# Output products of two gated layers in float16 parts, with divided high weights and low parts kept 1024 times larger

## The chip, the core and the metric

The kernel runs on one core of a Trainium2 chip. It uses five engines with queues of their own: TensorE (PE; a weight load is PEld), VectorE (DVE), ScalarE (ACT), GpSimd (POOL) and SyncE (SP), which issues the transfers here. An engine takes its instructions in the order of the program; a wait for another engine is a semaphore. The metric is the device time of one execution in microseconds.

## What is computed

```python
def _attn_ref(q, k, v, f):               # (4, 8, 576, 64), f: (4, 8, 576)
    scores = 1.0 / np.sqrt(D) * np.matmul(q, k.transpose(0, 1, 3, 2))
    cum = np.cumsum(np.log(np.clip(f, 0.0001, 1.0)), axis=-1)
    scores = np.where(causal, -1000000000.0, scores + cum[:, :, :, None] - cum[:, :, None, :])
    attn = softmax(scores)
    return np.matmul(attn, v)

def _moe_ref(x, w_a, w_b, w_out):        # 2304 tokens, 512 -> 1536 -> 512
    return ((x @ w_a) * (x @ w_b)) @ w_out

def _moe2_ref(x, w_in, w_out):           # 512 -> 2048 -> 512
    h = x @ w_in
    g = np.where(h >= 1, h, np.where(h <= -1, 0.0, (h + 1) ** 2 / 4.0))
    return g @ w_out
```

Attention over 32 heads (the kernel's 4 batches of 8 heads are cut in the reference's order), then the first layer (called the first mixture here), then the second. Inputs are float32 with a wide range of values; the weights come to the chip as pairs of 32-bit words that the kernel decodes to float32.

## The kernel before

**Products in parts.** A matmul of full precision is made of three: high weight by high activation, high weight by low activation, low weight by high activation (`mm3`, lines 590 to 594; in the profile L592, L593 and L594). For the input products (`whi_in`, `wlo_in`, activations `xh` and `xl` in the tile `xhl`) the parts are float16: a weight unit (four blocks of 128 x 128) is scaled by a power of two from its largest magnitude, `sc`, so that it fits; `winv` is the inverse scale. For the output products (`whi_out`, `wlo_out`, activations `ah`, `al`) the parts are float32 with the type fp32r, unscaled.

**Weights.** `weight_stream` decodes units in pairs: a transfer (`wraw`), two passes on ACT, three on DVE and one on POOL (`decode`, L509 to L519). For an input pair, the maximum of each unit (`wmx`, L568) is transposed on PE (L476), reduced on DVE, spread over all partitions by a small matmul on PE (L489), and inverted (`wsc`). `split_unit` then makes the parts: of an input unit ACT makes the high part (L534) and POOL scales (L535) and subtracts (L536); of an output unit POOL copies (L538) and subtracts (L539). The stream is advanced by `w_pump` every second tick of the main loop and whenever a block is asked for that is not there yet; finished units stand in rings, which `w_free` makes free.

**Items.** Tokens are cut into five spans of 460 or 464. An item is one group of hidden features by one span. In the first mixture (`moe1_item`, groups of two features' blocks) the two input products `oa` and `ob` are multiplied: ACT scales `oa` to `asb` (L652), DVE multiplies with `ob` (L653), ACT casts the result to `ah` (L654), POOL subtracts to get `al` (L655). In the second (`moe2_item`, groups of four) DVE clamps (L732), ACT squares (L733), DVE scales and takes the maximum (L734), ACT casts to `ah` (L735), POOL subtracts to `al` (L736); the scales of an item (`ih`, `ihalf`, `htop`, `hlow`) are operations of 4 columns on DVE (L720 to L723). The output products of an item (`out_part`) are issued within the next item: in the first mixture behind that one's first feature, in the second behind its third of four. `accumulate` adds them into `y` (DVE, L691 and L768; a copy on ACT for the first group) or, in the last group, writes the result out (L771).

**Order.** Up to the end of attention all instructions go through `Plan`, which collects them and issues them in an order that a model of the engines makes; where that model has PE idle it puts filler matmuls (`heat`, L1053, on a constant `mask`), and its instructions have the line L304. There one group of the first mixture for each batch, with spans of 288, is threaded between attention rounds. Behind it (`xpose` of the last batch, L1026 to L1037, then the items of all further groups) the tile framework's scheduler sets the order of each engine. Products of an item use six PSUM banks there; one while `Plan` orders.

Of the kernel before, what the change touches and what calls it, by code (L numbers as in the profile page):

```python
# [55 lines left out]
F64_MAX = 122864.0  # L56

# [267 lines left out]
def tile_decay_attention__then__moe__then__moe2(  # L325
# [45 lines left out]
    half = const.tile([P, 1], F32, name="half")  # L371
# [59 lines left out]
    def constants():  # L431
# [18 lines left out]
        nc.gpsimd.memset(half, 0.5)  # L450
# [71 lines left out]
    def split_unit(u, m):  # L522
        k = kind(u)
        while not free[k]:
            yield False
        free[k] -= 1
        p = slot(k)
        dt = F16 if k == "in" else F32R
        hi = p.tile([P, UB, P], dt, name=f"whi_{k}", tag=f"whi_{k}")
        lo = p.tile([P, UB, P], dt, name=f"wlo_{k}", tag=f"wlo_{k}")  # L530
# [12 lines left out]
    def weight_stream():  # L543
# [5 lines left out]
        for u0 in range(0, NU + 2, 2):  # L549
            new = wdec_p.tile([P, 2, UB * P], F32, name="wm", tag="wm") if u0 < NU else None  # L550
            scaled = u0 > 0 and kind(u0 - 2) == "in"
# [14 lines left out]
            if u0 < NU and kind(u0) == "in":  # L566
# [10 lines left out]
    def w_block(i):  # L577
# [3 lines left out]
        hi, lo = ws[u]  # L581
        return hi[:, i % UB, :], lo[:, i % UB, :]
# [22 lines left out]
    def act_pair(nt):  # L605
        return tuple(env["act"].tile([P, env["width"]], F32R, name=n, tag=n)[:, :nt] for n in ("ah", "al"))
# [27 lines left out]
    def scale_of(u, b):  # L634

        if (u, b) not in xw:
            t = xw_p.tile([P, 2], F32, name="xw", tag="xw")
            nc.vector.tensor_scalar(t, winv[:, u:u + 2], xinv[:, b:b + 1], None, ALU.mult)
            xw[u, b] = t
        return xw[u, b]  # L640

    def moe1_item(g, b, c0, nt, last_use):
# [5 lines left out]
        def epilogue(oa, ob, ic):  # L648
# [3 lines left out]
            nc.scalar.activation(asb, oa, AF.Copy, scale=ic[:, 0:1])  # L652
            after(4, lambda: nc.vector.scalar_tensor_tensor(pr, ob, ic[:, 1:2], asb, ALU.mult, ALU.mult))  # L653
            after(5, lambda: nc.scalar.copy(ah, pr))  # L654
# [539 lines left out]
```

## Time and profile before

| | |
|---|---|
| median of 3 runs | 1058.06 us |
| lowest, highest | 1055.68 us, 1067.14 us |
| span of the profiled execution | 1063.1 us |
| PE matmul, busy | 1034.0 us, 97% of the span |
| PE weight load, busy | 736.8 us, 69% |
| DVE, busy | 712.5 us, 67% |
| ACT, busy | 510.9 us, 48% |
| POOL, busy | 543.0 us, 51% |
| granted PE clock, mean | 0.984 of full speed |

The profile is of one execution. For that execution the page gives the span, from its first to its last instruction, and no time of another kind. Busy times count the durations of instructions, and those of successive matmuls overlap; how fast matmuls follow each other is read from their starts. A row of a group gives the busy time of all its instructions and their mean duration, then how long the engine stood idle just before them and what ended that. A row of the timeline gives start, duration, engine, line, operation, what is written and read, and the shape.

### The profile page before, as it was taken

Reading aid. Unit: us, or ns where it says so; the run is one execution under the profiler, and the core shown is the slowest. Engines: PE = TensorE matmul, PEld = TensorE weight load, DVE = VectorE, ACT = ScalarE, POOL = GpSimd, SP = SyncE. Lnnn points to the kernel's source line nnn. Section 1 sums busy time; section 2 is a strip of 40 time slices with the busy share of each in tenths; the row PEclk is TensorE's granted clock in tenths of the full one; section 3 lists DMA queues with packets and bytes.
Section 4 is the critical chain, followed back from the end, with each engine's and each line's share of the span. In section 5 each row is a group of like instructions: output and inputs, shape, how many; then the busy total and the mean of one; then the engine's idle time right before and its main releaser. Section 6 shows DMA issues by size and latency. Waiting matters only on the chain.

```text
span 1063.1 us, 17972 instructions
## 1 busy us (share of the span) xinstructions
PE 1034.0 (97%) x6799; PEld 736.8 (69%) x6799; DVE 712.5 (67%) x1584; ACT 510.9 (48%) x957; POOL 543.0 (51%) x516
## 2 busy tenths in 40 slices
PE   6999999889999999999999999999999999999998
PEld 5788888778765666666666666666766766767766
DVE  7699999977768663562753688964378567654342
ACT  4699888677654341331332444554445335223231
POOL 6388988654368651642723733732366347324121
PEclk8699999989999999999999999999999999999999
DMA  9454555321033220120210211010022011000101
GB/s 246 142 167 133 162 167 155 112 79 39 24 98 86 71 82 1 40 80 1 62 59 8 92 60 40 22 58 1 1 80 80 1 40 40 1 1 11 62 37 71
DMA packets 22054, 72.00 MB, mean 68 GB/s; under 512 B 2776, under 2 KB 5336, under 8 KB 21904
## 3 DMA queue, kind: packets, MB, share of 16 engines
q1 hardware_dynamic: 21968, 70.87, 22.2%
q8 instruction: 53, 0.87, 0.3%
q14 instruction: 33, 0.27, 0.1%
HBM read 60.26 MB, written 5.96 MB: 62 GB/s over the span
## 4 chain that ended last, share of the span: by engine, by line
PE 73%; DVE 15%; ACT 4%; issue 3%; DMA 3%; POOL 2%; SPq 0%; DVEq 0%; ACTq 0%; POOLq 0%
PE mm L592 21%; PE mm L594 20%; PE mm L593 20%; PE s L304 4%; DVE prob L304 3%; PE tp L304 3%; DVE tl L304 3%; PE mm L304 3%; PE o L304 2%; DMA wraw<-in_w_dram 1%; DVE xt L304 1%; DVE wm L516 1%; ACT prob L304 1%; DVE wm L512 1%; DVE wm L514 1%
## 5 line engine op out<-in xcount | busy, mean ns | idle before, releaser
L592 PE MATMUL mm<-xhl,whi_in 128*128 128x460 f16 (+2 forms) x752 | 266.8, 355 | 0.0
L593 PE MATMUL mm<-xhl,whi_in 128*128 128x460 f16 (+2 forms) x752 | 266.5, 355 | 0.0
L594 PE MATMUL mm<-xhl,wlo_in 128*128 128x460 f16 (+2 forms) x752 | 266.5, 355 | 0.0
L592 PE MATMUL mm<-ah,whi_out 128*128 128x460 f32 (+2 forms) x536 | 198.6, 384 | 0.6 <-ACT ah L735 0.6
L736 POOL TENSOR_TENSOR al<-tmp,ah 128x460 fp32r<-128x460 f32 (+1 forms) x80 | 96.2, 1203 | 201.0 <-ACT ah L735 200.9
L593 PE MATMUL mm<-al,whi_out 128*128 128x460 f32 (+2 forms) x536 | 197.8, 370 | 0.8 <-POOL al L736 0.8
L594 PE MATMUL mm<-ah,wlo_out 128*128 128x460 f32 (+2 forms) x536 | 197.6, 370 | 0.0
L655 POOL TENSOR_TENSOR al<-tmp,ah 128x460 fp32r<-128x460 f32 (+2 forms) x54 | 64.9, 1203 | 139.5 <-ACT ah L654 121.0
L592 PEld LDWEIGHTS <-whi_in 128*128 128x128 f16 x752 | 73.4, 98 | 75.1 <-issue 9.4
L594 PEld LDWEIGHTS <-wlo_in 128*128 128x128 f16 x752 | 73.5, 98 | 69.5
L593 PEld LDWEIGHTS <-whi_in 128*128 128x128 f16 x752 | 73.6, 98 | 64.7 <-issue 0.2
L733 ACT ACTIVATE tmp<-tmp,half,ihalf 128x460 f32<-128x460 f32 (+1 forms) x80 | 61.7, 771 | 113.3 <-DVE tmp L732 109.1
L592 PEld LDWEIGHTS mm<-ah,whi_out 128*128 128x128 f32 x536 | 100.4, 188 | 15.7 <-ACT ah L735 1.0
L593 PEld LDWEIGHTS mm<-al,whi_out 128*128 128x128 f32 x536 | 100.7, 188 | 12.3 <-POOL al L736 1.1
L519 POOL TENSOR_TENSOR wm<-wm,wr 128x512 int32<-128x512 int32 x58 | 75.4, 1300 | 64.9 <-DVE wm L516 48.1
L594 PEld LDWEIGHTS mm<-ah,wlo_out 128*128 128x128 f32 x536 | 100.7, 188 | 10.8
L653 DVE SCALAR_TENSOR_TENSOR tmp<-mm,xw,tmp 128x460 f32<-128x460 f32 (+2 forms) x54 | 36.7, 680 | 97.8 <-PE mm L594 96.5
L734 DVE SCALAR_TENSOR_TENSOR tmp<-mm,ih,tmp 128x460 f32<-128x460 f32 (+1 forms) x80 | 55.5, 694 | 51.8 <-ACT tmp L733 49.4
L732 DVE TENSOR_SCALAR tmp<-mm,htop,hlow 128x460 f32<-128x460 f32 (+1 forms) x80 | 59.9, 749 | 43.0 <-PE mm L594 42.7
L304 ACT ACTIVATE prob<-prob,nm 128x512 f32<-128x512 f32 (+4 forms) x144 | 80.4, 586 | 14.2 <-DVE nm L304 13.0
L735 ACT CAST ah<-tmp 128x460 fp32r<-128x460 f32 (+1 forms) x80 | 46.1, 576 | 66.5 <-DVE tmp L734 58.4
L304 PE MATMUL tp<-ident,prob 128*128 128x128 f32 x400 | 74.5, 291 | 2.5 <-ACT prob L304 0.8
(163 smaller groups left out, 2040.6 us busy)
## 6 DMA issues: line engine op xcount, KB each, us to landing
wraw<-in_w_dram SPq DMA_DIRECT2D x68, 512.0 KB
raw<-in_qk_dram SPq DMA_DIRECT2D x26, 608.0 KB
vraw<-in_v_dram SPq DMA_DIRECT2D x16, 320.0 KB
qk<-q SPq DMA_DIRECT2D x28, 160.0 KB
out_dram<-tmp SPq DMA_DIRECT2D x16, 230.0 KB
cum_d<-xhl SPq DMA_DIRECT2D x1, 1216.0 KB
y<-in_qk_dram SPq DMA_DIRECT2D x2, 608.0 KB
out_dram<-tmp SPq DMA_DIRECT2D x4, 232.0 KB
```

The costliest lines, as they stand in the source:

```text
L304: getattr(getattr(self.nc, engine), method)(*a, **kw)
L519: nc.gpsimd.tensor_tensor(t, t, r, ALU.add)
L592: nc.tensor.matmul(o, lhsT=wh, rhs=xh, start=first, stop=False)
L593: nc.tensor.matmul(o, lhsT=wh, rhs=xl, start=False, stop=False)
L594: nc.tensor.matmul(o, lhsT=wl, rhs=xh, start=False, stop=last)
L653: after(4, lambda: nc.vector.scalar_tensor_tensor(pr, ob, ic[:, 1:2], asb, ALU.mult, ALU.mult))
L655: after(6, lambda: nc.gpsimd.tensor_tensor(al, pr, V(ah), ALU.subtract))
L732: nc.vector.tensor_scalar(t, o, top[:, m], low[:, m], ALU.min, ALU.max)
L733: after(1, lambda: nc.scalar.activation(t, t, AF.Square, scale=ihalf[:, m], bias=half))
L734: after(2, lambda: nc.vector.scalar_tensor_tensor(r, o, ih[:, m], t, ALU.mult, ALU.max))
L735: after(3, lambda: nc.scalar.copy(ah, r))
L736: after(4, lambda: nc.gpsimd.tensor_tensor(al, r, V(ah), ALU.subtract))
```

## The change

Weights of the output products are now scaled and split as those of the input products are, both parts in float16. A third tile, `wdown`, is the high part divided by 1024 (`LOW`), made on DVE. `mm3` takes it for the product with the low activation. Activations are scaled by a bound that is known before the product (for the first mixture from the weights' scales, `group1`; for the second from `group2` and the span's scale), `ah` is float16 and holds the activation divided by 1024, `al` is float16 and holds what remains, not divided. `split_act` makes them with two scaled copies on ACT and the subtraction on POOL. `accumulate` multiplies by a scale (`out_scale1`, `osc`). The scales of an item of the second mixture are made by five operations on DVE and six on POOL.

```diff
+LOW = 2.0 ** 10
...
-    half = const.tile([P, 1], F32, name="half")
...
-        dt = F16 if k == "in" else F32R
...
-        if k == "in":
-            sc = wsc[:, u:u + 1]
-            nc.scalar.activation(hi, t, AF.Copy, scale=sc)
-            nc.gpsimd.tensor_scalar(t, t, sc, 0.0, ALU.mult, ALU.add)
-            nc.gpsimd.tensor_tensor(lo, t, hi, ALU.subtract)
-        else:
-            nc.gpsimd.tensor_scalar(hi, t, 1.0, 0.0, ALU.mult, ALU.add)
-            nc.gpsimd.tensor_tensor(lo, t, V(hi), ALU.subtract)
-        ws[u] = (hi, lo)
+        sc = wsc[:, u:u + 1]
+        nc.scalar.activation(hi, t, AF.Copy, scale=sc)
+        nc.gpsimd.tensor_scalar(t, t, sc, 0.0, ALU.mult, ALU.add)
+        nc.gpsimd.tensor_tensor(lo, t, hi, ALU.subtract)
+        down = hi
+        if k == "out":
+            down = p.tile([P, UB, P], F16, name="wdown", tag="wdown")
+            nc.vector.tensor_scalar(down, hi, 1.0 / LOW, None, ALU.mult)
+        ws[u] = (hi, lo, down)
...
-            scaled = u0 > 0 and kind(u0 - 2) == "in"
+            scaled = u0 > 0
...
-            if u0 < NU and kind(u0) == "in":
+            if u0 < NU:
                 mx = const2.tile([P, 2], F32, name="wmx", tag="wmx")
...
-        wh, wl = wb
+        wh, wl, wd = wb
         nc.tensor.matmul(o, lhsT=wh, rhs=xh, start=first, stop=False)
-        nc.tensor.matmul(o, lhsT=wh, rhs=xl, start=False, stop=False)
+        nc.tensor.matmul(o, lhsT=wd, rhs=xl, start=False, stop=False)
         nc.tensor.matmul(o, lhsT=wl, rhs=xh, start=False, stop=last)
...
+    def split_act(ah, al, r, spare, delay):
+        def high():
+            nc.scalar.activation(ah, r, AF.Copy, scale=1.0 / LOW)
+            nc.scalar.activation(spare, ah, AF.Copy, scale=LOW)
+
+        after(delay, high)
+        after(delay + 1, lambda: nc.gpsimd.tensor_tensor(al, r, spare, ALU.subtract))
...
+    def out_scale1(g, b):
+        if ("o", g, b) not in xw:
+            u = base1[g] // UB + 4
+            t, o = small("ot", 2), small("os", 2)
+            nc.vector.tensor_scalar(t, group1(g)[0], xinv[:, b:b + 1], 2.0 ** 31, ALU.mult, ALU.mult)
+            nc.vector.tensor_scalar(t[:, 0:1], t[:, 0:1], t[:, 1:2], 2.0, ALU.mult, ALU.mult)
+            nc.vector.tensor_scalar(o, winv[:, u:u + 2], t[:, 0:1], None, ALU.mult)
+            xw["o", g, b] = o
+        return xw["o", g, b]
...
-            after(5, lambda: nc.scalar.copy(ah, pr))
-            after(6, lambda: nc.gpsimd.tensor_tensor(al, pr, V(ah), ALU.subtract))
+            split_act(ah, al, pr, asb, 5)
...
+            w_block(ob + KC * nf - 1)
+            sc = out_scale1(g, b)
...
-            nc.vector.tensor_tensor(ys, o, ys, ALU.add)
+            nc.vector.scalar_tensor_tensor(ys, o, sc, ys, ALU.mult, ALU.add)
...
-        nc.vector.tensor_scalar(ih, winv[:, u0:u0 + 4], yinv[:, i:i + 1], None, ALU.mult)
...
+        nc.gpsimd.tensor_scalar(ih, winv[:, u0:u0 + 4], yi, 0.0, ALU.mult, ALU.add)
+        nc.vector.tensor_scalar(u, yi, group2(g), 1.0, ALU.mult, ALU.add)
...
         nc.vector.reciprocal(top, ih)
-        nc.vector.tensor_scalar(low, top, -1.0, None, ALU.mult)
-        nc.vector.tensor_scalar(ihalf, ih, 0.5, None, ALU.mult)
+        nc.gpsimd.tensor_scalar(low, top, -1.0, 0.0, ALU.mult, ALU.add)
+        nc.gpsimd.tensor_scalar(mid, rv, 16.0, 0.0, ALU.mult, ALU.add)
+        nc.gpsimd.tensor_scalar(ihalf, ih, rv, 16.0, ALU.mult, ALU.mult)
+        nc.gpsimd.tensor_scalar(full, ihalf, rv, 64.0, ALU.mult, ALU.mult)
...
-            after(3, lambda: nc.scalar.copy(ah, r))
-            after(4, lambda: nc.gpsimd.tensor_tensor(al, r, V(ah), ALU.subtract))
+            split_act(ah, al, r, t, 3)
...
+            nc.gpsimd.tensor_scalar(osc, winv[:, ob // UB:ob // UB + 4], v, v, ALU.mult, ALU.mult)
```

On PE, at the end of an output part in the last group of the second mixture, before (weights, then the input unit of the next products):

```order
L592 MATMUL mm<-ah,whi_out 128x460
L593 MATMUL mm<-al,whi_out 128x460
L594 MATMUL mm<-ah,wlo_out 128x460
L592 LDWEIGHTS whi_in_205
L592 MATMUL mm<-xhl,whi_in_205 128x464
L593 LDWEIGHTS whi_in_205
```

and at the same place now:

```order
L589 LDWEIGHTS whi_out
L589 MATMUL mm<-ah,whi_out 128x460
L590 LDWEIGHTS wdown
L590 MATMUL mm<-al,wdown 128x460
L591 LDWEIGHTS wlo_out
L591 MATMUL mm<-ah,wlo_out 128x460
L589 LDWEIGHTS whi_in_199
```

Each output matmul has a weight load of its own now, as the input matmuls had and have; the order of the three is the same, and the low activation meets `wdown`.

On ACT, within an item of the second mixture in the third of its four groups, where weights are decoded, before (`wm` is the decoded unit, `w` its maximum, `tmp` the clamped and squared activation):

```order
L733 ACTIVATE tmp<-tmp,half,ihalf 128x460
L492 COPY winv<-tp 128x2
L534 ACTIVATE whi_in<-wm_192,wsc 128x512 x2
L735 CAST ah<-tmp 128x460
L733 ACTIVATE tmp<-tmp,half,ihalf 128x460
```

and around an output unit in the same group now:

```order
L775 ACTIVATE tmp<-tmp,hmid,ihalf 128x460
L491 COPY winv<-tp 128x2
L531 ACTIVATE whi_out_215<-wm_186,wsc 128x512
L531 ACTIVATE whi_out_218<-wm_186,wsc 128x512
L636 ACTIVATE ah<-tmp 128x460
L775 ACTIVATE tmp<-tmp,hmid,ihalf 128x460
L637 ACTIVATE tmp<-ah 128x460
L636 ACTIVATE ah<-tmp 128x460
L637 ACTIVATE tmp<-ah 128x460
```

The cast has become two copies (L636 and L637), and between two of them the next item's square can stand; high parts of output units (L531 with `whi_out`) are ACT's now.

On POOL, where items of the third group run and no input unit is left to split, before:

```order
L736 TENSOR_TENSOR al<-tmp,ah 128x460 x6
L736 TENSOR_TENSOR al<-tmp,ah 128x464 x4
L736 TENSOR_TENSOR al<-tmp,ah 128x460 x2
L538 TENSOR_SCALAR whi_out<-wm_192 128x512
L539 TENSOR_TENSOR wlo_out<-wm_192,whi_out 128x512
```

and now:

```order
L640 TENSOR_TENSOR al<-tmp 128x460 x4
L795 TENSOR_SCALAR hos<-winv,hv 128x4 x2
L762 TENSOR_SCALAR hlow<-htop 128x4
L763 TENSOR_SCALAR hmid<-hrv 128x1
L764 TENSOR_SCALAR ihalf<-ih,hrv 128x4
L765 TENSOR_SCALAR hfull<-ihalf,hrv 128x4
L640 TENSOR_TENSOR al<-tmp 128x460
```

Between the four `al` of an item stand operations of 1 or 4 columns now, in the same queue.

## Rows read from the trace of the kernel before

**Rows 1.** The page's first row: span of the profiled execution.
```profile
span 1063.1 us, 17972 instructions
```

**Rows 2.** Stretches: us, then each engine's busy us (instructions), PE clock, DMA share, GB/s.
```profile
0.00:283.00 283.00, 260.40 (x2892) 218.83 (x2893) 247.19 (x795) 212.94 (x445) 187.40 (x200) 0.94 0.45 132
60.00:220.00 160.00, 148.61 (x1809) 126.61 (x1808) 155.36 (x510) 132.78 (x285) 131.68 (x124) 0.99 0.49 148
283.00:655.00 372.00, 371.63 (x1921) 237.22 (x1919) 221.51 (x376) 141.66 (x258) 188.53 (x171) 1.00 0.18 54
655.00:707.00 52.00, 50.46 (x252) 31.68 (x251) 48.89 (x93) 29.67 (x54) 28.70 (x24) 1.00 0.20 61
707.00:1059.00 352.00, 351.54 (x1738) 249.02 (x1738) 194.06 (x321) 126.60 (x202) 138.41 (x123) 1.00 0.09 29
```

**Rows 3.** PE's waits, 275 us to end: what waited, for what, total us, times, longest.
```profile
PE mm L593 <- POOL al L736: 0.8, 1, 0.8
PE mm L592 <- ACT ah L735: 0.6, 1, 0.6
PE tp L489 <- ACT wdg L483: 0.5, 1, 0.5
```

**Rows 4.** Timeline of PE: start us, duration us, line, operation; first and last of three runs.
```profile
1016.97 0.37 PE L593 MATMUL mm<-al,whi_out 128*128 128x460 f32 x1
...
1026.52 0.37 PE L594 MATMUL mm<-ah,wlo_out 128*128 128x460 f32 x1
...
1029.08 0.36 PE L592 MATMUL mm<-xhl,whi_in 128*128 128x464 f16 x1
...
1035.93 0.36 PE L594 MATMUL mm<-xhl,wlo_in 128*128 128x464 f16 x1
...
1036.55 0.37 PE L594 MATMUL mm<-ah,wlo_out 128*128 128x460 f32 x1
...
1045.97 0.37 PE L594 MATMUL mm<-ah,wlo_out 128*128 128x460 f32 x1
```

**Rows 5.** Groups by form: line, tiles, shape, count, busy us, mean ns, idle before.
```profile
L592 PE MATMUL mm<-ah,whi_out 128*128 128x460 f32 x416 | 154.2, 385 | 0.6 <-ACT ah L735 0.6
...
L592 PE MATMUL mm<-ah,whi_out 128*128 128x464 f32 x104 | 40.3, 391 | 0.0
...
L304 PE MATMUL mm<-ah,whi_out 128*128 128x288 f32 x48 | 16.0, 333 | 0.1
```

**Rows 6.** Timeline of PE around one spreading matmul, three rows in succession.
```profile
796.62 0.36 PE L594 MATMUL mm<-xhl,wlo_in 128*128 128x460 f16 x1
796.91 0.17 PE L489 MATMUL tp<-wdg,ones 2*128 2x2 bf16 x1
797.01 0.37 PE L592 MATMUL mm<-xhl,whi_in 128*128 128x460 f16 x1
```

**Rows 7.** Groups by form of the nearest operations; last, one line's min/median/max in ns.
```profile
L735 ACT CAST ah<-tmp 128x460 fp32r<-128x460 f32 x64 | 36.8, 575 | 52.7 <-DVE tmp L734 47.2 <-PE mm L594 4.7 <-DVE w L480 0.8
...
L534 ACT ACTIVATE whi_in<-wm,wsc 128x512 f16<-128x512 f32 x36 | 24.6, 718 | 9.5 <-PE mm L593 9.4
...
L568 DVE TENSOR_REDUCE wmx<-wm 128x2 f32<-128x1024 f32 x17 | 20.7, 1215 | 8.8 <-POOL wm L519 8.8
...
L512 DVE TENSOR_SCALAR wm<-wm 128x512 f32<-128x512 f32 x58 | 40.6, 700 | 17.4 <-ACT wm L509 17.2
...
L720 DVE TENSOR_SCALAR ih<-winv,yinv x20: 208/221/1199, 631.5 to 974.3; 128x4 f32<-128x4 f32 x20
```

**Rows 8.** Timeline: fourth `al` on POOL and its first matmul on PE, two items.
```profile
822.94 1.18 POOL L736 TENSOR_TENSOR al<-tmp,ah 128x460 fp32r<-128x460 f32 x1 [4.20 <-ACT ah L735]
...
824.31 0.37 PE L593 MATMUL mm<-al,whi_out 128*128 128x460 f32 x1
...
1013.13 1.16 POOL L736 TENSOR_TENSOR al<-tmp,ah 128x460 fp32r<-128x460 f32 x1 [11.19 <-ACT ah L735]
...
1018.83 0.37 PE L593 MATMUL mm<-al,whi_out 128*128 128x460 f32 x1
```

More of the change, by code (lines that the diff above doesn't have):

```diff
@@ L580, in w_block @@
             assert w_pump()
-        hi, lo = ws[u]
-        return hi[:, i % UB, :], lo[:, i % UB, :]
+        return tuple(t[:, i % UB, :] for t in ws[u])
     def w_free(u):
@@ L605, in act_pair @@
     def act_pair(nt):
-        return tuple(env["act"].tile([P, env["width"]], F32R, name=n, tag=n)[:, :nt] for n in ("ah", "al"))
+        return tuple(env["act"].tile([P, env["width"]], F16, name=n, tag=n)[:, :nt] for n in ("ah", "al"))
     pending = []
@@ L632, in tile_decay_attention__then__moe__then__moe2, with small, group1, group2 @@
     base2 = [end1 + i * 4 * 2 * KC for i in range(len(G2))]
[L634 to L640, printed above, removed]
+    def small(name, n=1):
+        return xw_p.tile([P, n], F32, name=name, tag=name)
+    def split_act(ah, al, r, spare, delay):
[4 more added lines that the diff above has]
+        after(delay + 1, lambda: nc.gpsimd.tensor_tensor(al, r, spare, ALU.subtract))
+    def group1(g):
+        if ("g", g) not in xw:
+            u = base1[g] // UB
+            top, inv, q, r = small("gtop", 2), small("ginv", 2), small("gq", 4), small("gr", 2)
+            nc.vector.tensor_tensor(top, winv[:, u:u + 2], winv[:, u + 2:u + 4], ALU.max)
+            nc.vector.reciprocal(inv, top)
+            for i in range(2):
+                nc.vector.tensor_tensor(q[:, 2 * i:2 * i + 2], winv[:, u + 2 * i:u + 2 * i + 2], inv, ALU.mult)
+                nc.vector.tensor_scalar(r[:, i:i + 1], q[:, 2 * i:2 * i + 1], q[:, 2 * i + 1:2 * i + 2], 2.0 ** -27,
+                                        ALU.mult, ALU.mult)
+            xw["g", g] = (top, r)
+        return xw["g", g]
+    def out_scale1(g, b):
[7 more added lines that the diff above has]
+        return xw["o", g, b]
+    def group2(g):
+        if ("k", g) not in xw:
+            u = base2[g] // UB
+            k = small("gk")
+            nc.vector.tensor_reduce(k, winv[:, u:u + 4], axis=AX.X, op=ALU.max)
+            nc.vector.tensor_scalar(k, k, 2.0 ** 39, None, ALU.mult)
+            xw["k", g] = k
+        return xw["k", g]
     def moe1_item(g, b, c0, nt, last_use):
@@ L646, in moe1_item, with epilogue @@
         acts = []
-        def epilogue(oa, ob, ic):
+        def epilogue(oa, ob, r):
             asb, pr = tmp(nt), tmp(nt)
@@ L764, in accumulate @@
             ys = y[:, c, cs]
+            sc = osc[:, c:c + 1]
             if g == 0:
-                nc.scalar.copy(ys, o)
+                nc.scalar.activation(ys, o, AF.Copy, scale=sc)
             elif g < len(G2) - 1:
-                nc.vector.tensor_tensor(ys, o, ys, ALU.add)
+                nc.vector.scalar_tensor_tensor(ys, o, sc, ys, ALU.mult, ALU.add)
             else:
                 t = tmp(nt)
-                nc.vector.tensor_tensor(t, o, ys, ALU.add)
+                nc.vector.scalar_tensor_tensor(t, o, sc, ys, ALU.mult, ALU.add)
                 nc.sync.dma_start(out=out[c * P:(c + 1) * P, cs], in_=t)
@@ L1125, in tile_decay_attention__then__moe__then__moe2 @@
     xw_p = pool("xw2", 4)
+    xw.clear()
     env["pt"] = pool("ps_t2", 2, space=bass.MemoryType.PSUM)
```

31 lines of the change are left out of this document (18 added, 13 removed).

## The prediction

> **What bounds the kernel now.** I read the page first, then the busy time by stretches, then what TensorE waits for, then its timeline matmul by matmul. The page gives a span of 1063.1 us [rows 1]. The stretches divide it: up to 283 us (attention, with the first group of the first mixture threaded in) PE has 260.4 of 283 us and DVE 247.2; from 283 us to 1059 us PE has 371.6 of 372, 50.5 of 52 and 351.5 of 352 [rows 2]. After 275 us the waits of PE that the profile can name are of 0.8, 0.6 and 0.5 us, once each [rows 3]. So the last three quarters of the kernel last exactly as long as PE's own stream of matmuls, and a change there is worth what it does to the pace of that stream. Ahead of 283 us the bound is mixed: from 60 us to 220 us DVE is the fullest engine (155.4 of 160 us) [rows 2].
>
> The reader should then see two paces in that stream. In a run of output products with fp32r operands, 47 matmuls of 460 columns start between 1016.97 and 1026.52 us: 46 steps in 9.55 us, 207.6 ns each; in the next run, 1036.55 to 1045.97 us, 45 steps take 209.3 ns each. Input products in float16, 464 columns wide, take 35 steps from 1029.08 to 1035.93 us: 195.7 ns each, which is 194.0 ns for 460 columns [rows 4]. The duration that a group shows for one matmul (385 ns) overlaps its neighbours and is not the pace [rows 5].
>
> **What the change removes.** Every output product becomes a float16 matmul with a weight load of its own, three per block as before. Taking 208.5 ns as the mean of the two fp32r runs, one wide output matmul is shortened by 14.5 ns. There are 416 + 104 of each of three kinds [rows 5], 1560 in all, and the loads do not come out as extra time, because the float16 input products already carry one load per matmul and still run at 194 ns. That is 22.6 us. 64 narrow ones (288 columns) after 283 us at the same saving give 0.9 us. Together −23.5 us, all of it on the engine that sets the end. Of the 48 narrow ones per kind ahead of that [rows 5], the same saving would be 2 us, if PE set the end there.
>
> Here the page "TensorE: Matmul & The Clock Gate" of the Trainium skill, section "Back-to-back issue gap", speaks against the change: warm matmuls follow each other every N/2.4 + 2.5 ns, and no type of operand is in it, so that fp32r and float16 should run alike. For 460 columns that is 194.2 ns, which this trace agrees with for float16, and disagrees with for fp32r; by the page the −23.5 us would be nothing.
>
> **What it adds on TensorE.** Output weights are now scaled as the input weights are, so each pair of output units brings a transpose of its maxima and a small spreading matmul. The order of the two programs holds 30 such pairs of the later kind where it held 17: 13 more. One spreading matmul between input products stretches a step of 0.195 us to 0.39 us (796.62 to 797.01 us) [rows 6], a pause of 0.195 us; I put the transpose between nothing and the same, so a pair costs 0.195 to 0.39 us, and I take 0.3: 13 × 0.3 = +3.9 us (2.5 to 5.1).
>
> **What it adds on the other engines, after 283 us.** For each of 130 activations ScalarE now does two scaled copies where it did one cast of 575 ns [rows 7]: about 75 us more over 776 us, in which ScalarE was busy 298 us [rows 2]; no bound, but a longer chain from the last input product of an item to the low part `al` that the output product needs. An output unit goes from a GpSimd copy to a ScalarE copy (718 ns), and VectorE gets the maximum of each pair (1215 ns) and the divided weight `wdown`; no row has that operation, the nearest is a scaling of as many float32 elements on VectorE, 700 ns on the mean [rows 7]. I keep 0 and 1.4 us (twice that row) as ends, and 0.7 as value. The four small steps of a spread come to 4 × 0.22 = 0.9 us at the median of the small scaling `ih` [rows 7]. For 13 pairs that is 13 × (1.2 + 2 × 0.7 + 0.9) = 13 × 3.5 = 45 us of VectorE beside 776 us, in which it has 464 us [rows 2]. Accumulating with a scale, and the cost of the raised maxima, lie beside PE's matmuls in the same way. If that cover were gone, what waits is PE at the first use of a weight.
>
> What can come out on PE is a wait for `al`. In a quiet item the fourth `al` ends at 1014.29 us and its matmul starts at 1018.83 us, 4.5 us later; while weights are decoded, one ends at 824.12 us for a matmul at 824.31 us, 0.2 us later [rows 8]. The added copy takes about 0.6 us of that. The timeline has 20 items of the second mixture; the last is ordered in another way, and of the other 19 five have less than 3 us to spare. None late is 0; all 20 late by 0.6 us is 12 us. From 655 us to 707 us VectorE is busy 48.9 of 52 us [rows 2]; two pairs of output units passing there add 2 × 3.5 = 7 us, which can be put off to the emptier stretch behind it, or be met by PE. I take 3.5 us for both, close to the end with slack, since 14 of the 19 items have it: +3.5 (−1.9, if the present waits go, to 12).
>
> **Up to 283 us.** VectorE gets one pair of output units (3.5 us) and some 14 more small scalings (0.22 us at the median of `ih`) [rows 7]: 6.6 us, of which a part lies where VectorE is 97% busy. Of the fillers that the program's planner puts where it expects PE idle, the order holds 183 instead of 139, which says that PE's work there moves, not what it costs. ScalarE gets 28 narrow copies. PE may give back 2 us. Between −2 and +7 us I take +2, since the end of this stage, from 220 us on, is PE's again.
>
> **Sum.** −23.5 + 3.9 + 3.5 + 2 = −14.1 us. The profiled span of 1063.1 us becomes 1049.0. That span lies within the runs shown (1055.68 to 1067.14 us), 5.0 us over their median of 1058.06; taken off the median, 1044.0 us.
>
> **Rivals.**
> *All hidden.* No `al` late, the present waits gone, PE's gain kept up to 283 us: −23.5 + 2.5 − 1.9 − 2 = −24.9, or 1033 us. For it: slack of over 4 us in most items. Against: the stretch from 655 us, where VectorE has no room.
> *Given back.* PE's stream is shorter, but its waits take it: −23.5 + 5.1 + 12 + 7 = +0.6, or 1059 us. For it: VectorE at 97% in 60 to 220 us and 94% in 655 to 707 us.
> *Slower: GpSimd's small operations hold up `al`.* Each item of the second mixture now has five operations of 4 columns on GpSimd ahead of its fourth `al`, in one queue. No row has them; the same scaling on VectorE takes 208 to 1199 ns, half of them up to 221 [rows 7]. If each took 1.2 us, 6 us plus 0.6 of copy would exceed the 4.5 us of slack by 2.1 us in each of 20 items: 42 us, and with the rest −14.1 + 42 = +28, 1086 us. It decides from 1.6 us an item, that is from about 1.1 us for one such operation. Against it: GpSimd waits for the cast ahead of the `al` in most items, and the small ones need not wait for it.
> The page "SBUF — State Buffer" of the Trainium skill, section "SBUF: two separate sides", says that VectorE and GpSimd take one shared pair of ports by turns, each for a whole instruction; no row here tells which of two held the other, but the spread of the small scaling would fit it.
> *No gain in pace.* If the pace of the output products did not follow their type, what is added would stay alone: 3.9 + 3.5 + 2 = +9.4, or 1067 us. Against it: the two paces of one trace, 14.5 ns apart, ten microseconds apart. That rival is the rule of the skill's page on TensorE, above.
>
> **How the numbers follow.** The forecast, 1044 us with its own range of 1038 to 1051, gets 0.50; all hidden 0.17; given back 0.20; slower 0.08; no gain in pace 0.05. A change of 1%, 10.6 us, is about what a measurement of this kernel can tell from none: faster means below 1047.5 us, slower above 1068.6 us. Three quarters of the forecast's own chance and all of "all hidden" lie below: 0.375 + 0.17, or 0.55. Slower takes the 0.08 of its rival and a little of the two next to it: 0.10. The rest, 0.35, is within 1%. The range runs from all hidden to given back, 1033 to 1059 us, and leaves out the two last rivals and some of the edges.
>
> **What would show it.** Right: output matmuls of 460 columns that start 194 ns apart; PE without idle time between 283 us and the end but for a few microseconds near the change from the first to the second mixture; last PE instruction some 16 us earlier counted from the first input product behind attention. Wrong: waits of PE for `al` in many items (slower, or given back), waits of PE on the spreading matmuls, a first stage longer than 290 us, or output matmuls still at 208 ns. The forecast would fall with the first stage above all, whose order of instructions is remade as a whole and which no row of before can tell.

## The result, and the profile after

The changed kernel takes 1051.47 us at the median of 18 runs (1038.03 to 1057.21), the kernel before 1058.11 us over 18 runs on the same chip (1055.68 to 1068.0). The ratio is 0.990, 95% interval 0.987 to 0.993. Medians here are over all runs, while a ratio leaves disturbed runs out and is not the quotient of the medians; where the two differ, the text says so.

The time lies inside the range, 7.5 us above the forecast of 1044.0. The profiled run of the changed kernel took 1044.85 us, and that agreement is half chance, as the experiments show. Its page begins with the span (before: [rows 1]) and the busy time of each engine:

```profile
span 1043.1 us, 18612 instructions
PE 1010.7 (97%) x6871; PEld 594.1 (57%) x6871; DVE 736.0 (71%) x1761; ACT 600.4 (58%) x1159; POOL 584.7 (56%) x635
```

The stretches, with the columns of [rows 2] (us, then busy us of PE, PEld, DVE, ACT, POOL with their instructions, PE clock, DMA share, GB/s):

```profile
0.00:281.00 281.00, 257.32 (x2939) 213.21 (x2939) 253.10 (x817) 219.81 (x461) 188.76 (x199) 0.96 0.46 133
60.00:220.00 160.00, 147.05 (x1720) 123.12 (x1719) 152.98 (x492) 132.53 (x283) 121.51 (x115) 0.97 0.46 137
281.00:655.00 374.00, 373.40 (x1984) 191.40 (x1982) 243.71 (x479) 175.73 (x341) 192.81 (x182) 1.00 0.18 54
655.00:700.00 45.00, 41.77 (x214) 20.39 (x213) 39.90 (x96) 32.27 (x62) 35.83 (x40) 1.00 0.16 47
700.00:1039.00 339.00, 338.26 (x1741) 169.15 (x1739) 198.61 (x371) 172.55 (x298) 167.25 (x216) 1.00 0.10 34
```

Behind 281 us PE is still full, and the engines beside it have room, VectorE 243.7 of 374 us and 198.6 of 339. The pace of the output products is the one that was forecast. Timeline of PE, the first and the last of 41 output matmuls in succession, and the input product behind them (before: [rows 4]):

```profile
999.71 0.36 PE L590 MATMUL mm<-al,wdown 128*128 128x460 f16 x1
...
1007.48 0.36 PE L591 MATMUL mm<-ah,wlo_out 128*128 128x460 f16 x1
1007.67 0.36 PE L589 MATMUL mm<-xhl,whi_in 128*128 128x460 f16 x1
```

That is 40 steps in 7.77 us, 194.3 ns each, against 207.6 and 209.3 ns in [rows 4]; the change of kind at 1007.67 us no longer changes the pace. The groups by form (before: [rows 5] and [rows 7]) have as many matmuls as before, and beside them the added work, `wdown` among it, at 387 ns on the mean:

```profile
L589 PE MATMUL mm<-ah,whi_out 128*128 128x460 f16 x416 | 139.0, 357 | 0.5 <-DVE tmp L776 0.5
...
L636 ACT ACTIVATE ah<-tmp 128x460 f16<-128x460 f32 x104 | 60.7, 584 | 86.8 <-DVE tmp L686 45.6 <-DVE tmp L776 36.4 <-PE mm L591 1.8
L637 ACT ACTIVATE tmp<-ah 128x460 f32<-128x460 f16 x104 | 60.6, 583 | 2.3
...
L537 DVE TENSOR_SCALAR wdown<-whi_out 128x512 f16<-128x512 f16 x26 | 10.0, 387 | 4.9 <-ACT whi_out L531 4.8
```

What PE waits for behind 275 us (what waited, for what, total us, times, longest; before: [rows 3]):

```profile
PE mm L589 <- DVE tmp L776: 1.7, 3, 1.2
PE mm L590 <- POOL al L640: 1.0, 1, 1.0
PE mm L1097 <- ACT y L305: 0.9, 1, 0.9
PE tp L488 <- ACT wdg L482: 0.8, 2, 0.6
```

One wait for `al` is left in the whole stream (662.96 us), none in an item behind 700 us.

Since several parts of the kernel move at once, all profiles below are cut at the same four places, read from the timelines: the end of the 19th of attention's 144 exponential instructions (the expectations on record count from zero and call it the 18th), of the 55th and of the 73rd, and the start of the first input product behind attention, which is the stage's end. The stream is from there to the end of PE's last instruction.

```
kernel        19th exp  55th to 73rd  19th to stage's end  stage's end   stream
before            56.9          26.6                226.0        283.0    775.8
before, again     50.2          26.6                227.5        277.7    775.8
changed           48.9          35.0                232.0        280.9    757.4
changed, again    61.8          37.0                232.0        293.8    756.8
```

The stream is 18.4 us shorter (757.4 for 775.8), more than the 16.1 us that I had for it. From the 19th exponential to the stage's end the changed kernel needs 4.5 to 6 us more. Against b_again it is +1.0 us up to the 55th, +8.4 from there to the 73rd, and −5.0 behind, part of which is decoding that is now done earlier (the second output unit is cast at 138.1 us in b_again, before 124 us in the changed kernel). How long the first 18 take moves by 13 us between two profiles of the same program. The experiments take these three apart.

### The profile page after: what moved, and what is told of

It is laid out like the page before. It is cut to its first block, busy times and chain, and to the rows that moved or that the text cites. A ratio compares the mean times of both kernels' runs of the same rounds, so it can differ in the third digit from the quotient of the medians.

```text
span 1043.1 us, 18612 instructions
## 1 busy us (share of the span) xinstructions
PE 1010.7 (97%) x6871; PEld 594.1 (57%) x6871; DVE 736.0 (71%) x1761; ACT 600.4 (58%) x1159; POOL 584.7 (56%) x635
## 4 chain that ended last, share of the span: by engine, by line
PE 70%; DVE 19%; ACT 3%; POOL 3%; issue 3%; DMA 2%; SPq 0%; DVEq 0%; ACTq 0%; POOLq 0%
PE mm L589 21%; PE mm L590 20%; PE mm L591 20%; DVE prob L305 3%; DVE tl L305 3%; PE s L305 2%; PE mm L305 2%; PE tp L305 2%; PE o L305 1%; DMA vraw<-in_v_dram 1%; DVE xt L305 1%; DVE xhl L1091 1%; DVE xhl L741 1%; DVE wm L305 1%; DMA y<-y 1%
## 5 line engine op out<-in xcount | busy, mean ns | idle before, releaser
L640 POOL TENSOR_TENSOR al<-tmp 128x460 f16<-128x460 f32 (+2 forms) x134 | 159.7, 1193 | 192.7 <-ACT tmp L637 183.5
L590 PE MATMUL mm<-al,wdown 128*128 128x460 f16 (+2 forms) x536 | 190.1, 356 | 1.0 <-POOL al L640 1.0
L591 PE MATMUL mm<-ah,wlo_out 128*128 128x460 f16 (+2 forms) x536 | 190.1, 356 | 0.0
L589 PE MATMUL mm<-ah,whi_out 128*128 128x460 f16 (+2 forms) x536 | 178.8, 356 | 0.5 <-DVE tmp L776 0.5
L636 ACT ACTIVATE ah<-tmp 128x460 f16<-128x460 f32 (+2 forms) x134 | 77.7, 580 | 107.2 <-DVE tmp L776 49.4
L775 ACT ACTIVATE tmp<-tmp,hmid,ihalf 128x460 f32<-128x460 f32 (+1 forms) x80 | 60.9, 761 | 76.6 <-DVE tmp L774 76.5
L776 DVE SCALAR_TENSOR_TENSOR tmp<-mm,hfull,tmp 128x460 f32<-128x460 f32 (+1 forms) x80 | 55.6, 694 | 60.6 <-ACT tmp L775 56.7
L305 ACT ACTIVATE prob<-prob,nm 128x384 f32<-128x384 f32 (+4 forms) x144 | 80.7, 583 | 16.8 <-DVE nm L305 16.1
L637 ACT ACTIVATE tmp<-ah 128x460 f32<-128x460 f16 (+2 forms) x134 | 77.6, 579 | 3.0
L725 DVE SCALAR_TENSOR_TENSOR y<-mm,os,y 128x460 f32<-128x460 f32 (+1 forms) x100 | 64.8, 688 | 20.0 <-PE mm L591 19.9
```

Source lines behind the costliest of these rows:

```text
L305: getattr(getattr(self.nc, engine), method)(*a, **kw)
L590: nc.tensor.matmul(o, lhsT=wd, rhs=xl, start=False, stop=False)
L591: nc.tensor.matmul(o, lhsT=wl, rhs=xh, start=False, stop=last)
L636: nc.scalar.activation(ah, r, AF.Copy, scale=1.0 / LOW)
L637: nc.scalar.activation(spare, ah, AF.Copy, scale=LOW)
L640: after(delay + 1, lambda: nc.gpsimd.tensor_tensor(al, r, spare, ALU.subtract))
```

## The experiments

**The same kernel again (b_again).** The kernel before, unchanged, for a second profile.

> The kernel before, unchanged, for a second profile and for the granted clock beside each run's time, which the first runs of it do not give. Theory A (the change shortens the stream behind attention by 18 us and lengthens the attention stage by 7 to 11 us, because that stage's order and VectorE's work are remade): this kernel's attention stage ends, by the start of the first matmul 464 columns wide, at about 290 to 298 us, and its stretch from there to the end is 765 us again, within 1 us. Theory B (the attention stage costs nothing; what the two profiles differ by there is the chance of the clock in each run): the attention stage of this kernel moves from run to run by 10 us or more, with the granted clock, as the changed kernel's does (its runs go from 1038 to 1057 us).

It took 1059.28 us (ratio 1.003, 1.000 to 1.006). Between its two profiles the stream is 775.8 us both times, 55th to 73rd exponential 26.6 us both times; only what lies ahead of the 19th exponential differs much, 56.9 and 50.2 us. (The mark of the expectation, the first wide input product, which is 460 columns wide, comes at 298.4 and 293.1 us, and 760.4 and 760.5 us follow.) The ten runs go from 1055.59 us at a granted clock of 0.992 to 1067.58 us at 0.980. So both theories hold a part: the clock moves the start of the stage from run to run, and the stages behind it can be compared between single profiles to within 1.5 us.

**The type alone, behind attention (pace2).**

```diff
-        dt = F16 if k == "in" else F32R
+        dt = F32R if k == "out" and u < 6 else F16
...
-            ah, al = act_pair(nt)
+            ah, al = act_pair(nt, g > 0)
```

> The kernel before with the output products of every group but the first of the first mixture cast to float16 parts, and nothing else: no scales, no divided weights (what it leaves out is the range of the numbers, so its output is not the reference's). The attention stage has the order of before. If the type alone sets the pace of those matmuls, as I costed it: 1560 wide matmuls at 194 instead of 208.5 ns, 22.6 us less, or 1035.5 us where the kernel before takes 1058.1 (a ratio of 0.979), and output matmuls of 460 columns that start 194 ns apart. If what a float16 product gains needs the rest of the change, or comes from elsewhere: 1058 us. Theories A and B agree here on the 0.979.

1036.64 us, ratio 0.981 (0.976 to 0.987). The stream takes 753.9 us: 21.9 less, where the sum had 23.5, and the output matmuls of 460 columns start 194.2 ns apart on the mean. Float16 operands alone carry the whole gain. Their weight loads are shorter too, first in the kernel before, then in pace2:

```profile
L592 PEld LDWEIGHTS mm<-ah,whi_out 128*128 128x128 f32 x536 | 100.4, 188 | 15.7 <-ACT ah L735 1.0 <-ACT ah L654 0.2
```
```profile
L598 PEld LDWEIGHTS <-whi_o 128*128 128x128 f16 x520 | 50.9, 98 | 50.3 <-issue 1.1
```

The load does not set the pace, though: in the kernel before, fp32r matmuls of 288 columns, with the same loads of 188 ns, follow each other in 133 ns (nine steps between these two rows).

```profile
293.02 0.29 PE L592 MATMUL mm<-ah,whi_out 128*128 128x288 f32 x1
...
294.22 0.29 PE L592 MATMUL mm<-ah,whi_out 128*128 128x288 f32 x1
```

**The threaded group left as it was (g0_old).** With `NEW1` as the groups of the first mixture that get the new form:

```diff
+NEW1 = (1, 2, 3, 4, 5)
+NEW2 = True
...
+        return kind(u) == "in" or (u // 6 in NEW1 if u < n else NEW2)
```

> The changed kernel with the one group that is threaded into attention (the first of the first mixture) left in the fp32r form of before; the other five groups and the whole second mixture in the new form. Its instructions in the attention stage stand in the order of before on every engine, 139 fillers. Theory A: the stage is that of before, the stream behind it that of the change: 1058.1 - 18.3 + 0.7 (its two narrow items stay slow) = 1040.5 us, a ratio of 0.983 to before, and 7 to 11 us faster than the changed kernel. Theory B: as the changed kernel, a ratio of about 0.990 (1047.5 to 1051.5 us).

1039.46 us, ratio 0.983 (0.979 to 0.987), 12 us below the changed kernel by the medians and 7 by the ratios. The stream is 757.3 us, as in the changed kernel, and 55th to 73rd exponential is 26.6 us, as in the kernel before. Theory A's number was 1040.5.

**The threaded group alone in the new form (g0_new).** The same, with `NEW1 = (0,)` and `NEW2 = False`.

> The kernel before with only the one group that is threaded into attention in the new form (scaled float16 parts, its pair of output units with maximum, spread and divided weight, 28 more narrow copies on ScalarE); everything behind attention as before. The planner remakes the order of the attention stage for it, with 176 fillers before the first wide matmul. Theory A: the attention stage becomes 7 to 11 us longer and nothing else changes: 1058.1 + 7 to 11 = 1065 to 1069 us, a ratio of 1.007 to 1.010. Theory B: 1057 to 1060 us, a ratio of 0.999 to 1.002.

1071.51 us, ratio 1.012 (1.009 to 1.015). The stream is that of before (775.8 us), 55th to 73rd exponential 35.9 us. The new form of this one group, two of 28 units of output weights, costs 12 to 14 us by the medians of the two experiments, 7 and 13 us by their ratios. That is more than the 4.5 to 6 us of the table, so something else is in it.

**Which part of it (lot3, g0_pace, g0_act, g0_dve).** The new form brings three things to the attention stage: another order of everything, more copies on ScalarE, more work on VectorE. The first two were made without the third, and the third without the second. The order: `PORT = 10.0` became `9.0` in the planner. The type without new work: the diff of pace2 the other way round, float16 for `u < 6` only. ScalarE's copy, on top of that:

```diff
+            def high():
+                nc.scalar.copy(ah, pr)
+                nc.scalar.copy(asb, ah)
```

and VectorE's work without the copy, from g0_new, with the new split of two weight units on ScalarE and GpSimd still in it:

```diff
-            nc.scalar.activation(ah, r, AF.Copy, scale=1.0 / LOW)
-            nc.scalar.activation(spare, ah, AF.Copy, scale=LOW)
+            nc.scalar.copy(ah, r)
...
-        after(delay + 1, lambda: nc.gpsimd.tensor_tensor(al, r, spare, ALU.subtract))
+        after(delay + 1, lambda: nc.gpsimd.tensor_tensor(al, r, ah, ALU.subtract))
```

> The kernel before with one weight of its planner changed (PORT from 10 to 9), so that the same instructions of the attention stage stand in another order on every engine, as far from the order of before as the changed kernel's is by the eye; 142 fillers instead of 139. No work is added or taken. It tells what a remade order is worth by itself. Theory C (the attention stage grows because VectorE has more to do in it): 1056 to 1061 us, as before. Theory D (it grows because the planner's new order is a worse one, by chance): a shift of 4 us or more against 1058 us, in either direction. Theory E (it grows by ScalarE's second copies): as C.

> The kernel before with the output products of the one group that is threaded into attention cast to float16 parts, and nothing else (no scales, no divided weights, no second copy: the range of the numbers is left out). All else is fp32r as before. The planner remakes the order of the attention stage, since these products cost less, with no new work on VectorE or ScalarE. Theory C: 1055 to 1058 us (PE saves up to 2.8 us with 192 narrow matmuls of 14.5 ns). Theory D: off by 4 us or more. Theory E: as C. The kernel with the whole new form in this group took 1071.5 us.

> As the kernel with the threaded group cast to float16 parts, plus the second copy on ScalarE that the change adds to each activation of that group (28 copies of 288 columns, one for each activation of the stage): GpSimd subtracts the copy instead of the high part. No work is added on VectorE; the scales and the divided weights are left out. Theory C: 1055 to 1060 us. Theory E: 1065 to 1071 us, most of what the whole new form cost (1071.5 us). Theory D: another number again, with no rule.

> The kernel before with the threaded group in the new form but without the second copy on ScalarE (the low part is taken from the high part as it stands, so it is not enlarged and the output is not the reference's): VectorE has all that the change gives it there (the maximum of the pair of output units, its spread, the two divided weights, the group's and the batches' small scalings). Theory C: 1067 to 1072 us, as the whole new form (1071.5). Theory E: 1056 to 1060 us. Theory D: another number again, with no rule.

```
kernel    median   ratio (95%)            19th exp  55th to 73rd  19th to stage's end  stream
lot3      1061.54  0.9995 (0.995, 1.004)      55.9          28.3                224.2   776.4
g0_pace   1063.50  1.001 (0.998, 1.005)       56.6          26.7                227.7   775.4
g0_act    1060.36  1.001 (0.998, 1.004)       49.3          26.7                228.5   775.5
g0_dve    1071.78  1.011 (1.008, 1.014)       49.1          39.1                235.1   779.0
g0_new    1071.51  1.012 (1.009, 1.015)       56.7          35.9                232.5   775.8
```

Only the kernels with VectorE's added work have the long stretch between the 55th and the 73rd exponential, and g0_dve has all of the loss without ScalarE's copies: theory C holds and theory E falls. (In its profile PE waits 2.1 us for VectorE in that stretch and 2.6 us once in the stream, and behind each wait the clock is at its lower level for 3.4 us, hence 39.1 and 779.0.) That it is VectorE's share of the new form, and not the split on the other two engines, is read from the stretch below. Theory D falls by the ratios, but not by the medians: lot3 and g0_pace lie 4 and 6 us above before, and in 7 and 6 of their 10 runs the granted clock was below 0.986, which 6 of 31 runs of before beside them had. g0_act, whose order is remade too, had one in 10. At the same granted clock neither is slower: lot3 took 1061.4 to 1062.6 us at 0.981 and 0.982, g0_pace 1062.9 to 1065.8, runs of before 1066.3 to 1067.2 at 0.982; g0_new took 1070.1 and 1071.1 us there. So an order can make a low clock more frequent, and need not.

The stretch itself, first in the kernel before (b_again), then the changed kernel, then g0_act:

```profile
101.60:128.20 26.60, 24.96 (x325) 21.63 (x324) 25.67 (x90) 22.01 (x49) 24.53 (x24) 1.00 0.55 169
```
```profile
101.40:136.40 35.00, 32.35 (x406) 26.78 (x407) 34.38 (x117) 27.99 (x62) 30.26 (x29) 1.00 0.52 150
```
```profile
101.10:127.80 26.70, 26.11 (x314) 21.88 (x314) 25.80 (x90) 23.43 (x51) 24.94 (x25) 1.00 0.63 183
```

VectorE is busy 97% of it in b_again and 98% in the changed kernel. It has 8.7 us more to do there, 34.38 for 25.67, and the stretch is 8.4 us longer. Most of what it does more stands in its timeline (start us, duration us, line, operation):

```profile
114.16 1.04 DVE L305 TENSOR_TENSOR gtop<-winv 128x2 f32<-128x2 f32 x1
...
116.12 1.04 DVE L305 TENSOR_TENSOR gq<-winv,ginv 128x2 f32<-128x2 f32 x1
...
117.32 1.21 DVE L305 TENSOR_REDUCE wmx<-wm 128x2 f32<-128x1024 f32 x1
...
120.33 0.16 DVE L305 TENSOR_TENSOR gq<-winv,ginv 128x2 f32<-128x2 f32 x1
...
122.69 0.69 DVE L305 TENSOR_SCALAR ot<-gtop,xinv 128x2 f32<-128x2 f32 x1
...
125.73 1.46 DVE L305 TENSOR_SCALAR wdown<-whi_out 128x512 f16<-128x512 f16 x1
...
127.23 0.50 DVE L305 TENSOR_SCALAR wdown<-whi_out 128x512 f16<-128x512 f16 x1
...
133.50 1.16 DVE L305 TENSOR_SCALAR os<-winv,ot 128x2 f32<-128x2 f32 x1
```

These eight are 7.3 us. The operation `gq` stands there twice, on tiles of two columns both times: once 1.04 us and once 0.16. GpSimd's timeline at the same times:

```profile
113.91 1.27 POOL L305 TENSOR_TENSOR wm<-wm,wr 128x512 int32<-128x512 int32 x1 [0.73 <-DVE wm L305]
...
115.78 1.36 POOL L305 TENSOR_TENSOR vl<-vraw,vh 128x640 f16<-128x640 f32 x1
...
120.49 0.81 POOL L305 TENSOR_TENSOR al<-tmp,tmp 128x288 f16<-128x288 f32 x1 [1.74 <-DVE gq L305]
...
133.21 1.42 POOL L305 TENSOR_TENSOR qk<-raw,k 64x576 fp32r<-64x576 f32 x1
```

`gtop` begins during GpSimd's 113.91 us instruction and ends with it (115.20 and 115.18 us); the long `gq` ends with the next (117.16 and 117.14); `os` ends with a third (134.66 and 134.63). The short `gq` ran while GpSimd stood idle. These rows fit what "SBUF — State Buffer" of the Trainium skill, section "SBUF: two separate sides", states, that VectorE (in a mode with two ports, or with two inputs in SBUF) and GpSimd share a pair of ports, which one of them holds for a whole instruction while the other stands still. The same is seen wherever these small operations stand ahead of 283 us (`xw`, `gtop`, `gq`, `ot` and `os` on two columns, 75 of them in seven profiles: before, b_again, after, a_again, after_heat, g0_new, g0_dve): all 39 that took 0.24 us or more began during a GpSimd instruction and ended within 0.03 us of the end of one, and the 30 that began with GpSimd idle took 0.14 to 0.23 us. (The other six began during one and took no longer than 0.22.) The rows show the ends to coincide; no run here took GpSimd's work away to prove the cause. The kernel before pays the same price for its own small scaling, which the change removes:

```profile
107.99 0.96 DVE L304 TENSOR_SCALAR xw<-winv,xinv 128x2 f32<-128x2 f32 x1
```

**The first 18 exponentials (a_again, after_heat, g0_old_heat, before_heat).** What was left was that the changed kernel's runs had a granted clock of 0.979 to 0.985 in 16 of 18, where 25 of 31 runs of before had 0.986 or more. a_again is the changed kernel once more; in the other three, 40 more fillers stand on PE ahead of the first score matmul:

```diff
+            if cold and engine == "tensor" and a and a[0].tensor.name.startswith("s_"):
+                cold = False
+                for _ in range(EXTRA):
+                    self.heat()
```

> The changed kernel, unchanged, for a second profile. So far its runs took 1051.5 us at the median with a granted clock of 0.979 to 0.985 in 16 of 18, while the kernel before had 0.986 or more in 25 of 31. Theory F (a second loss of the attention stage, beside VectorE's work: the early stretch at the lower level of the clock is longer under the new order): a profile at 0.98 shows that stretch near 19 us lasting 20 us or more where the profile of 1044.85 us showed 10.2, and the 18th exponential ending at 55 us or later instead of 48.9. Theory G (the clock differs elsewhere): the 18th exponential ends at 49 to 51 us all the same. Either way 1050 to 1053 us.

> The changed kernel with 40 more fillers on PE (matmuls of a zero tile that nothing reads) put ahead of the first score matmul, where PE stands idle from about 13.4 to 18 us; nothing else is moved. Theory F, with the idle time at 13.4 to 18 us as what the clock's fall follows: the early stretch at the lower level goes or gets shorter, most runs at 0.99 or more, 1040 to 1045 us. If that idle time has nothing to do with it: 1050 to 1053 us and 0.98 as without them.

> The changed kernel with the threaded group left in the form of before (1039.5 us) and the same 40 more fillers ahead of the first score matmul. If the idle time ahead of it is what the clock's fall follows: 5 to 7 us less where the early stretch of 10 to 14 us goes altogether, 1033 to 1036 us. If it is not: 1039 to 1040 us.

> The kernel before with the same 40 more fillers ahead of the first score matmul. It tells what the change is worth where the early stretch at the lower level of the clock is mostly gone: the changed kernel with these fillers took 1042.7 us. If the change costs 8 to 10 us of VectorE's work in the attention stage and gives 18 us behind it, with the clock apart from both: 1051 to 1054 us (1058 less 4 to 6 for a stretch of 10 to 14 us at half the rate), 9 to 11 us above the changed kernel. If the clock were not apart (fillers help the changed kernel only): 1057 to 1059 us.

```
kernel        median   ratio (95%)            19th exp  19th to stage's end  stream
changed       1051.47  0.990 (0.987, 0.993)       48.9                232.0   757.4
a_again       1049.30  0.991 (0.987, 0.995)       61.8                232.0   756.8
after_heat    1042.71  0.983 (0.978, 0.989)       52.4                230.1   756.8
g0_old_heat   1034.98  0.975 (0.968, 0.983)       44.4                226.8   757.3
before_heat   1053.38  0.996 (0.993, 0.9995)      44.2                226.3   776.3
```

Theory F holds. Busy times by stretches (columns as above; the clock is the third number from the end), first a_again, then the changed kernel's other profile, then before_heat:

```profile
10.00:17.00 7.00, 4.09 (x43) 3.83 (x40) 6.96 (x11) 2.65 (x3) 6.34 (x8) 1.00 1.04 220
17.00:58.00 41.00, 40.67 (x212) 28.63 (x213) 24.58 (x77) 21.58 (x43) 15.37 (x15) 0.51 0.54 151
58.00:100.00 42.00, 40.72 (x504) 34.10 (x502) 40.80 (x145) 37.97 (x80) 35.03 (x33) 0.99 0.54 161
```
```profile
10.00:18.00 8.00, 3.57 (x37) 3.35 (x35) 7.96 (x12) 2.29 (x3) 7.09 (x8) 1.00 1.01 209
18.00:29.00 11.00, 11.00 (x31) 7.66 (x31) 6.03 (x20) 6.64 (x11) 2.55 (x2) 0.53 0.86 247
29.00:100.00 71.00, 68.48 (x841) 55.65 (x840) 68.48 (x245) 64.00 (x136) 58.14 (x56) 1.00 0.54 158
```
```profile
10.00:18.00 8.00, 8.00 (x87) 8.00 (x84) 7.96 (x11) 2.71 (x4) 7.21 (x10) 1.00 1.03 223
18.00:29.00 11.00, 10.11 (x77) 7.26 (x76) 10.69 (x35) 9.20 (x19) 1.72 (x2) 1.00 0.95 263
```

In both profiles of the changed kernel the clock falls to about 0.5, the level of 1.2 GHz, right behind an idle stretch of PE, and PE is full while it lasts: 10 us in one run, 41 us in the other, of the same program. In the two profiles of the kernel before it lasts 27 and 14 us. The timeline shows the idle stretch, ahead of the first score matmul, in the changed kernel, then in the kernel before (b_again):

```profile
17.83 0.68 PE L305 MATMUL s<-y 66*128 66x128 f32 x3 [4.43 <-DMA y<-y]
```
```profile
19.27 1.20 PE L304 MATMUL s<-y 66*128 66x128 f32 x3 [4.88 <-DMA y<-y]
```

With it filled, the granted clock of 11 of 12 runs of before_heat was 0.99 or more, and 0.995 the median, and after_heat's four had 0.989 to 0.997. In the profile of after_heat the clock still fell, from 23 us on and for 17 us, so the fillers make it rarer and do not rule it out. One of before_heat's runs still had 0.983 and took 1065.43 us. The gain is 4.5 us for the kernel before (1057.88 measured beside it) and 7 to 9 us for the changed one (1049.30 and 1051.47 without). With fillers in both, the change is worth 10.7 us, 1042.71 for 1053.38, from 4 and 12 runs on two chips. The stretch at the lower level is thus a loss of its own, larger under the order of the changed kernel. Why it is larger there stays open: the idle stretch is not longer (4.43 and 4.88 us), its length does not order what follows (3.25 us of it stand ahead of the 41 us in a_again, 6.32 ahead of the 27 us in the first profile of before), and g0_act's remade order did not have it more often.

g0_old_heat beats both kernels, 1034.98 us, and is 4.5 us below g0_old. One of its four runs took 1051.20 us at a granted clock of 0.980, so the low clock is not ruled out there either.

## Why the prediction was right in one half and wrong in the other

**Pace: right.** −23.5 us was the term; the type alone gave 21.9 in the stream, and output matmuls start 194.3 ns apart. The rival by which the pace would not follow the type has fallen on the same kernel: pace2 changes the type and, with it, only the number of buffers. That was the rule of the Trainium skill's "TensorE: Matmul & The Clock Gate", section "Back-to-back issue gap" (N/2.4 + 2.5 ns, no type in it): float16 keeps to it, 194.2 ns worked out by the page and 194.3 measured, fp32r at 208 does not. The section gives this formula for a matmul by itself and says that in a stream of weight loads and matmuls of 512 columns the spacing is shorter, 131 ns; the streams here, at 194 ns, do not show that. The narrow matmuls save 10.5 ns each (133 to 122.5 ns at 288 columns) and not the 14.5 of the sum, a difference of 0.3 us.

**New pairs: right.** I had 13 at 0.3 us, 3.9 us. Behind 300 us the trace has 28 spreading matmuls of the weights for 16, with a pause of 0.20 us each and 0.11 for their transposes: 12 × 0.31 = 3.7 us.

**Waits for `al` and the change of mixture: too high.** I had +3.5 us. Pace (−21.9) and pairs (+3.7) make −18.2 and the stream moved by −18.4, so the waits cost nothing on balance: PE is idle for 3.2 us between 655 and 700 us, where it was 1.5 in [rows 2]; by this sum as much has gone elsewhere, which no row shows singly. The rivals that hung on `al` (given back by late items; GpSimd's small operations ahead of it) have fallen: `al` is waited for once, 0.95 us. (The threshold set for the second was mis-summed: 10.5 us above the kernel before is 24.6 us above the sum of −14.1, or 1.2 us in each of 20 items, not 1.6.)

**Up to 283 us: the term that failed.** I took +2 us. It is +4.5 to 6 us behind the 19th exponential, and some 6 us more ahead of it in a typical run. Two steps were wrong.
The first is the place of VectorE's work. I counted 6.6 us and let only a part of it lie where VectorE is full. The amount was near, as the busy time from the 19th exponential to the stage's end shows, 207.22 us in the kernel before and 213.62 in the changed one (207.30 and 215.75 in their second profiles):

```profile
56.90:283.00 226.10, 211.64 (x2541) 181.44 (x2537) 207.22 (x681) 181.20 (x388) 157.22 (x149) 0.98 0.39 116
```
```profile
48.90:280.90 232.00, 215.02 (x2574) 179.94 (x2573) 213.62 (x704) 188.43 (x403) 157.94 (x148) 0.98 0.39 113
```

Two errors in it met. I priced the small scalings at 0.22 us, the median of `ih` in the second mixture [rows 7], where those with GpSimd at work beside them took up to 1.24 us in the changed kernel; and I did not take off `xw`, which goes away. The row to read was that one, 0.54 us on the mean in that very stage and up to 0.97:

```profile
L304 DVE TENSOR_SCALAR xw<-winv,xinv 128x2 f32<-128x2 f32 x6 | 3.1, 539 | 0.0
```

But most of the work stood in one stretch where VectorE had 3% to spare, so 8.7 us of busy time there became 8.4 us of delay, of which some 3.5 to 5 came back behind the stretch. PE's gain in that stage (2 us in the sum) does not show: g0_pace, which has it alone, needs 227.7 us from the 19th exponential on, before 226.0 and 227.5.
The second has no term in the sum at all: the clock. [rows 2] show it, 0.94 up to 283 us and 0.99 from 60 to 220 us, so nearly all of the loss lies ahead of 60 us. I read the column and did not ask what sets it, and took an order that is remade as a whole to be neutral there. The prediction did name the first stage as what could fail it.

**The sum.** −18.4 in the stream, +4.5 to 6 behind the 19th exponential, make −12.4 to −13.9; the median moved by 6.6, so the first 18 exponentials took the other 6 to 7 us. The clock of the runs says the same. Over the 74 runs of the kernel before that stand beside the experiments, the time falls by 1.06 us for each 0.001 of granted clock (1069 us at 0.980, 1056 at 0.992). The median run of the changed kernel has 0.983, that of before 0.990: 7 us, as an estimate from these runs. At an equal clock of 0.990 the changed kernel took 1044.85 and 1045.47 us (the second in a_again), before 1057.6 at the median of 48 runs. So at equal clock the change is worth 12 to 13 us, close to the 14.1 of the sum, and the clock takes about half of it back. The forecast of −14.1 was met in the profiled run of 1044.85 us because its early stretch at the lower level was a short one, with the 19th exponential 13 us ahead of a_again's. Only 2 of the 18 runs had the clock of 0.990 or more that is usual in the kernel before; that the profile fell on one of them is luck. Of the 6 to 7 us the fillers give back 2 to 4 (7 to 9 in the changed kernel less 4.5 in the other); for the rest the four runs of after_heat, one of them with a long stretch, tell too little.

## What to carry to other kernels

Price a small operation from the stage in which it will stand, not from a median over the kernel: an operation on two columns took 0.16 us beside an idle GpSimd and 1.04 us beside a busy one. Price what goes away, too, and ask in which stretch the rest will stand. When a change speeds up one engine everywhere, leave out the stages which another engine bounds; leaving one group of ten in its old form was worth 12 us of 1051 by the medians and 7 by the ratios. And a stage with PE idle at its start can lose more to the clock than the change is worth, by another amount in each run: compare stages between profiles, set runs of equal granted clock side by side, and put work into the idle stretch before judging the rest.

## What the runs showed of the hardware

The stretch at 1.2 GHz begins between 17 and 20 us in the profiles without the fillers and lasted 10 and 41 us in two runs of the same program, with PE busy 100% and 99% of it. A shorter one, 6.8 to 10.2 us in all, lies between 180 and 270 us in every profile, with fillers or without; nothing here explains it. Forty matmuls on a zero tile that nothing reads, in 4.4 to 4.9 us in which PE waited for a load, took 4.5 to 9 us off the medians of two whole kernels. Fp32r and float16 matmuls of 460 columns differ in pace, 209.1 to 194.2 ns on the mean, in programs that differ behind attention only in this type and in the number of buffers (before and pace2); at 288 columns it is 133 to 122.5 ns (before and after).
